# The last chunk of a fused attention and feed-forward kernel: h products first, then output products block by block, with the last block in two halves

## The chip, the cores and the metric

The kernel runs on one core of one Trainium2 chip. The metric is the device time of one execution, in microseconds (us). Engines: PE (TensorE, matmul), DVE (VectorE), ACT (ScalarE), POOL (GpSimd), SP (SyncE, which only issues transfers here).

## The reference, cut to what matters

```python
def reference(q, k, v, w_in, w_out, beta):       # q, k, v: 8 x 8 x 576 x 64
    x = linear_attention(q, k, v)                # cut; gives 4608 tokens x 512
    h = x @ w_in                                 # 512 -> 2048
    g = h * (1.0 / (1.0 + np.exp(-beta * h)))
    return (g @ w_out).astype(np.float32)        # 2048 -> 512
```

## The kernel before

Tokens are handled in 9 chunks of 512. The 2048 columns of `h` make 16 *units* of 128. For each unit, PE makes an `h` product (four matmuls of 128x512 into one PSUM bank), ACT takes a tanh, DVE makes `g`, and PE uses `g` for the *output products*: one matmul for each of four token *blocks* of 128, added up over the 16 units in four PSUM banks `acc0` to `acc3`. At the end each block is copied from PSUM (where matmuls put their results) to SBUF (on-chip memory, from which stores leave) by ACT or DVE, and stored. The code is shortened; `...` marks cuts.

```python
def mm_a(c, j, kts=None, tag=None):              # h product of unit j
    ...                                          # tag "h": two banks; "att": two more
    th = work.tile([P, MAIN], BF16, tag="th", bufs=3)
    nc.scalar.activation(th[:], h[:], ACTF.Tanh, scale=beta_t[:, j : j + 1])
    g = work.tile([P, MAIN], BF16, tag="g", bufs=6)
    nc.vector.scalar_tensor_tensor(out=g[:], in0=th[:], scalar=1.0, in1=h[:], op0=ALU.add, op1=ALU.mult)

def mm_b(c, j, sts=range(R)):                    # output products of unit j, R = 4 blocks
    for st in sts:
        nc.tensor.matmul(acc[st][:], g[:, ds(st * P, P)], w_out_b[:, j, :], start=(j == 0), stop=(j == NJ - 1))

def store(c, st): ...                            # for the last chunk:
    evac(nc.scalar if st in (0, 3) else nc.vector, o[:, st, :], acc[st][:])
    (nc.scalar if st == R - 1 else nc.sync).dma_start(ov[:, st, :], o[:, st, :])

# ... last chunk: h of unit j, output products of unit j - 2, up to j = 13; h of unit 14; then
mm_a(LASTC, NJ - 1, tag="att")
last = [(0, j) for j in range(NJ - 4, NJ - 1)] + [(1, j) for j in range(NJ - 4, NJ - 1)]
last += [(0, NJ - 1), (1, NJ - 1)] + [(st, j) for st in (2, 3) for j in range(NJ - 4, NJ)]
for st, j in last:
    mm_b(LASTC, j, [st])
    if j == NJ - 1:
        store(LASTC, st)
```

The softmax here doesn't subtract the row's maximum and nothing guards it: scores larger than these inputs give would overflow.

## Time and profile before

| | before |
|---|---|
| median of 5 runs | 288.95 us (288.61 to 289.18) |
| profiled span | 286.8 us |
| PE busy | 277.9 us, 97% |
| granted PE clock | full in all 40 slices |

The page of before, its line of PE, its chain of waits by engine, and the two groups of matmuls that fill the time (busy us, mean ns of one, idle time ahead of them and what ended it):

```profile
PE 277.9 (97%) x1595; PEld 127.7 (45%) x1595; DVE 180.0 (63%) x280; ACT 162.9 (57%) x236; POOL 43.7 (15%) x58
...
PE 84%; DMA 11%; SPq 1%; POOL 1%; ACT 1%; issue 0%; DVE 0%; ACTq 0%
...
L358 PE MATMUL h<-xT,w_in_b 128*128 128x512 bf16 x576 | 146.1, 379 | 0.5 <-ACT xT L143 0.2
L386 PE MATMUL acc<-w_out_b,g 128*128 128x512 bf16 x576 | 145.9, 379 | 0.2 <-DVE g L370 0.2
```

PE is the bottleneck nearly everywhere. A group's mean of 379 ns is not the pace: matmuls overlap, and in a stream they start 0.216 us apart.

The timeline of before at its end (start us, duration us, engine, line, what, count; in brackets the idle time before and what ended it):

```profile
276.95 1.89 PE L358 MATMUL h<-xT,w_in_b 128*128 128x512 bf16 x8
277.00 0.69 DVE L370 SCALAR_TENSOR_TENSOR g<-th,h 128x512 bf16<-128x512 bf16 x1 [1.04 <-ACT th L368]
...
278.67 0.60 PE L386 MATMUL acc<-w_out_b,g 128*128 128x512 bf16 x2
278.73 0.69 DVE L370 SCALAR_TENSOR_TENSOR g<-th,h 128x512 bf16<-128x512 bf16 x1 [1.04 <-ACT th L368]
...
279.47 3.20 PE L386 MATMUL acc<-w_out_b,g 128*128 128x512 bf16 x14 [0.20 <-DVE g L370]
...
281.38 1.52 SPq L434 DMA_DIRECT2D out_dram<-o  x3
...
282.71 0.58 ACT L143 COPY o<-acc 128x512 f32<-128x512 f32 x1 [1.36 <-PE acc L386]
283.32 0.37 ACTq L434 DMA_DIRECT2D out_dram<-o  x1
```

At 278.67 PE runs two output products and then needs `g` of unit 14, which DVE ends only at 279.42. The third matmul starts at 279.47 instead of 278.67 + 2 x 0.216 = 279.10: 0.37 us lost. The last block is copied by ACT in 0.58 us, and its store is issued at 283.32.

The windows view of before over its end (window in us, its length, then busy us of PE, PE weight loads, DVE, ACT and POOL, with counts; then granted PE clock, the DMA engines' busy share and GB/s):

```profile
279.00:280.00 1.00, 0.80 (x5) 0.29 (x4) 0.82 (x2) 0.56 (x1) 0.00 (x0) 1.00 0.00 0
...
281.00:282.00 1.00, 1.00 (x6) 0.49 (x5) 0.83 (x2) 0.35 (x1) 0.00 (x0) 1.00 0.00 0
282.00:283.00 1.00, 0.67 (x4) 0.10 (x1) 0.54 (x1) 0.29 (x1) 0.00 (x0) 1.00 0.75 287
283.00:284.00 1.00, 0.00 (x0) 0.00 (x0) 0.00 (x0) 0.29 (x1) 0.00 (x0) 1.00 1.04 371
284.00:285.00 1.00, 0.00 (x0) 0.00 (x0) 0.00 (x0) 0.00 (x0) 0.00 (x0) 1.00 1.00 356
285.00:286.00 1.00, 0.00 (x0) 0.00 (x0) 0.00 (x0) 0.00 (x0) 0.00 (x0) 1.00 0.10 35
```

Before 282 no store of the last chunk moves any data. All four of them (1 MB) are issued within 2 us, from 281.38 to 283.32, and the DMA engines are full (share near 1) until 285. By the trace's packet records the data runs from 282.23 to 285.27, and the last store's own part from 284.29 to 285.27. The span ends 1.56 us after its last byte. The view of this last store (`--tile o --window 283:286.8`) gives the time from its issue to its landing, which is when its completion is signalled:

```profile
DMA to landing us min/median/max: 2.6/2.6/2.6
```

### The profile page before, as it was taken

The numbers are of one execution on the slowest core, as the hardware profiler recorded it, in microseconds if no ns is written. First come the engines' busy times: TensorE is split into PE (matmuls) and PEld (weight loads), VectorE is DVE, ScalarE is ACT, GpSimd is POOL, SyncE is SP. The second block draws the span as 40 slices with busy tenths as digits, with TensorE's granted clock in tenths as the row PEclk, the third lists the DMA queues.
The fourth block names the chain that finished last, engine by engine and source line by source line (L and its number), as shares of the span: only waits on it lengthen the run. The fifth ranks groups of instructions, "written<-read, shape, count | busy, mean of one in ns | idle before, by whom it ended". The sixth has DMA issues, their size and how long they took to land.

```text
span 286.8 us, 4132 instructions
## 1 busy us (share of the span) xinstructions
PE 277.9 (97%) x1595; PEld 127.7 (45%) x1595; DVE 180.0 (63%) x280; ACT 162.9 (57%) x236; POOL 43.7 (15%) x58
## 2 busy tenths in 40 slices
PE   7799999999999999999999999999999999999994
PEld 2444445444444444444444444444445444444441
DVE  7954597695477457855694469456954695464432
ACT  4763586683496448734773568356835563553341
POOL 4458833300030020001200030003000000000000
PEclk9999999999999999999999999999999999999999
DMA  7999999809933963296319911893270033005004
GB/s 242 377 385 387 371 388 321 280 2 264 280 151 76 313 164 146 46 331 175 127 33 270 269 74 76 194 268 119 115 220 2 1 149 73 0 0 149 0 0 146
DMA packets 56227, 50.08 MB, mean 175 GB/s; under 512 B 26240, under 2 KB 47760, under 8 KB 56208
## 3 DMA queue, kind: packets, MB, share of 16 engines
q1 hardware_dynamic: 56064, 49.56, 55.8%
q8 instruction: 12, 0.20, 0.3%
q10 hardware_dynamic: 144, 0.26, 0.3%
q14 instruction: 7, 0.06, 0.1%
HBM read 36.71 MB, written 9.44 MB: 161 GB/s over the span
## 4 chain that ended last, share of the span: by engine, by line
PE 84%; DMA 11%; SPq 1%; POOL 1%; ACT 1%; issue 0%; DVE 0%; ACTq 0%
PE acc L386 40%; PE h L358 39%; DMA w_in<-in_moe_w_in_dram 6%; DMA k_st<-in_k_dram 5%; PE x L314 2%; PE kv L276 2%; POOL w_in_b L145 1%; PE kv L264 0%; PE tp L250 0%; SPq L85 0%; SPq L106 0%; PE x L318 0%; ACT ek L158 0%; DVE g L370 0%; ACT th L368 0%
## 5 line engine op out<-in xcount | busy, mean ns | idle before, releaser
L368 ACT ACTIVATE th<-h,beta_t 128x512 bf16<-128x512 f32 x144 | 98.5, 687 | 102.6 <-PE h L358 100.7
L370 DVE SCALAR_TENSOR_TENSOR g<-th,h 128x512 bf16<-128x512 bf16 x144 | 97.9, 682 | 92.2 <-ACT th L368 90.7
L358 PE MATMUL h<-xT,w_in_b 128*128 128x512 bf16 x576 | 146.1, 379 | 0.5 <-ACT xT L143 0.2
L386 PE MATMUL acc<-w_out_b,g 128*128 128x512 bf16 x576 | 145.9, 379 | 0.2 <-DVE g L370 0.2
L386 PEld LDWEIGHTS <-g 128*128 128x128 bf16 x576 | 56.0, 98 | 67.9 <-DVE g L370 1.0
L358 PEld LDWEIGHTS <-w_in_b 128*128 128x128 bf16 x576 | 55.3, 98 | 67.7 <-issue 2.7
L145 POOL CAST va<-v_st 128x2048 bf16<-128x2048 f32 (+2 forms) x12 | 17.3, 1460 | 145.0 <-DMA v_st<-in_v_dram 145.0
L225 DVE TENSOR_REDUCE rq<-eq 128x16 f32<-128x1024 bf16 x18 | 21.6, 1198 | 2.3 <-ACT eq L214 2.3
L231 DVE TENSOR_TENSOR eq<-eq,rq 128x1024 bf16<-128x1024 bf16 x18 | 22.6, 1257 | 0.1
L214 ACT ACTIVATE eq<-q_st 128x1024 bf16<-128x1024 f32 x16 | 16.3, 1048 | 2.9 <-DMA q_st<-in_q_dram 2.9
L143 ACT CAST xT<-x 128x512 bf16<-128x512 f32 x20 | 11.6, 585 | 11.1 <-PE x L314 10.3
L169 ACT ACTIVATE ek<-k_st 128x1024 bf16<-128x1024 f32 x12 | 12.6, 1047 | 0.0
L145 DVE COPY o<-acc 128x512 f32<-128x512 f32 x18 | 11.6, 683 | 0.9 <-PE acc L386 0.9
L314 PE MATMUL x<-qsT,kvp 128*128 128x512 bf16 x32 | 11.7, 380 | 0.4 <-DVE kvp L309 0.2
L145 DVE CAST xT<-x 128x512 bf16<-128x512 f32 x16 | 10.9, 684 | 0.5 <-PE x L314 0.5
L143 ACT COPY o<-acc 128x512 f32<-128x512 f32 x18 | 9.7, 591 | 2.6 <-PE acc L386 2.6
L158 ACT ACTIVATE ek<-k_st 64x576 bf16<-64x576 f32 x16 | 10.9, 679 | 0.4
L450 PE MATMUL warm<-kvp 128*128 128x512 bf16 x34 | 9.9, 432 | 1.2 <-DVE kvp L478 1.2
L145 POOL CAST w_out_b<-w_out 128x1024 bf16<-128x1024 f32 x8 | 8.2, 1040 | 6.6 <-DMA w_out<-in_moe_w_out_dram 6.5
L309 DVE TENSOR_TENSOR kvp<-kv,rk 64x256 bf16<-64x256 f32 (+2 forms) x24 | 8.0, 333 | 0.6
L145 POOL CAST w_in_b<-w_in 128x1024 bf16<-128x1024 f32 x7 | 7.2, 1040 | 3.5 <-DMA w_in<-in_moe_w_in_dram 3.4
L450 PEld LDWEIGHTS <-kvp 128*128 128x128 bf16 x34 | 3.4, 108 | 5.3 <-issue 2.1
(38 smaller groups left out, 67.1 us busy)
## 6 DMA issues: line engine op xcount, KB each, us to landing
out_dram<-o SPq DMA_DIRECT2D x14, 512.0 KB, 3.4
q_st<-in_q_dram SPq DMA_DIRECT2D x6, 1024.0 KB, 6.5
k_st<-in_k_dram SPq DMA_DIRECT2D x6, 1024.0 KB, 9.1
v_st<-in_v_dram SPq DMA_DIRECT2D x6, 1024.0 KB, 10.5
w_in<-in_moe_w_in_dram SPq DMA_DIRECT2D x3, 1024.0 KB, 9.7
k_st<-in_k_dram SPq DMA_DIRECT2D x8, 288.0 KB, 7.6
q_st<-in_q_dram SPq DMA_DIRECT2D x4, 512.0 KB, 7.8
w_out<-in_moe_w_out_dram SPq DMA_DIRECT2D x4, 512.0 KB, 9.5
```

The lines of the kernel that those rows point to most:

```text
L143: eng.copy(dst, src)
L145: eng.tensor_copy(dst, src)
L169: nc.scalar.activation(ek[b][:, :, h, :].rearrange("p i h d -> p h i d"), k_st[b][:, h, 0 : R * D].rearrange("p h (i d) -> p h i d", i=R), ...
L214: nc.scalar.activation(eq[b][:, :, s * m : (s + 1) * m, :].rearrange("p i h d -> p h i d"), q_st[b][:, s * m : (s + 1) * m, :].rearrange(" ...
L225: nc.vector.tensor_reduce(rq[b][:, 0, :, h], eq[b][:, :, h, :], axis=AX.X, op=ALU.add)
L231: nc.vector.tensor_tensor(eq[b][:, :, h, :], eq[b][:, :, h, :], rq[b][:, 1, :, h].unsqueeze(3).to_broadcast((P, R, m, D)), ALU.mult,)
L314: nc.tensor.matmul(t[:], kvp[:, c, j, :], qsT[c][:, :, j, :])
L358: nc.tensor.matmul(h[:], w_in_b[:, kt, ds(j * P, P)], x_of(c)[:, kt, :], start=(kt == 0), stop=(kt == KT - 1),)
L368: nc.scalar.activation(th[:], h[:], ACTF.Tanh, scale=beta_t[:, j : j + 1])
L370: nc.vector.scalar_tensor_tensor(out=g[:], in0=th[:], scalar=1.0, in1=h[:], op0=ALU.add, op1=ALU.mult)
L386: nc.tensor.matmul(acc[st][:], g[:, ds(st * P, P)], w_out_b[:, j, :], start=(j == 0), stop=(j == NJ - 1),)
L450: nc.tensor.matmul(t[:, 0:cols], kvp[:, B - 1, 0, :], kvp[:, B - 1, :, :].rearrange("p j r -> p (j r)")[:, 0:cols],)
```

## The change

The intent: PE should not wait for the last `g`, the blocks should end one after the other so that each is stored while PE still works on the next, and the last piece to be copied and stored should be small. The `h` products of units 10 to 15 run back to back, the output products of units 8 to 15 are held back and then follow block by block, and block 3 is two halves of 256 columns in two PSUM banks. (The Trainium skill, "PSUM — Partial Sum Buffer", section on bank collisions, says that two engines must not touch one bank's same quadrant at once. That is why the first half can be copied while PE fills the second only if they lie in two banks. The trace of after agrees as far as it goes: the copy of the first half runs from 281.95 to 282.37, and PE works on the second half until 282.79.) The diff, cut to its core:

```diff
-        g = work.tile([P, MAIN], BF16, tag="g", bufs=6, name=f"g{c}_{j}")
+        g = work.tile([P, MAIN], BF16, tag="g", bufs=10, name=f"g{c}_{j}")
 ...
+            if c == LASTC:
+                acc_of[c].append(ps.tile([P, DM], F32, tag="att", bufs=2, name=f"acc{c}_{R}"))
 ...
+            if c == LASTC and st >= R - 1:
+                hw = DM // 2
+                nc.tensor.matmul(
+                    acc[st][:, 0:hw],
+                    g[:, ds((R - 1) * P, P)],
+                    w_out_b[:, j, ds((st - R + 1) * hw, hw)],
+                    start=(j == 0), stop=(j == NJ - 1),
+                )
+                continue
 ...                                         # store(), last chunk
+            if st >= R - 1:
+                ...
+                evac((nc.vector, nc.scalar)[k_], o[:, R - 1, cols], acc[st][:, 0:hw])
+                (nc.sync, nc.scalar)[k_].dma_start(ov[:, R - 1, cols], o[:, R - 1, cols])
+                return
+            evac(nc.scalar if st == 1 else nc.vector, o[:, st, :], acc[st][:])
+            nc.sync.dma_start(ov[:, st, :], o[:, st, :])
 ...                                         # the last chunk's order
+    HOLD = 8
-                mm_a(c, j)
+                mm_a(c, j, tag="att" if n == B and j > HOLD + LAG and j % 3 == 0 else None)
+            if n == B and j >= HOLD + LAG:
+                continue
 ...
-    (the list `last` and its loop)
+    for st in range(R + 1):
+        for j in range(HOLD, NJ):
+            mm_b(LASTC, j, [st])
+        store(LASTC, st)
```

More of the change, by code (lines that the diff above doesn't have):

```diff
@@ L379, in acc_tiles, with mm_b @@
             ]
+            if c == LASTC:
+                acc_of[c].append(ps.tile([P, DM], F32, tag="att", bufs=2, name=f"acc{c}_{R}"))
         return acc_of[c]
-    def mm_b(c, j, sts=range(R)):
+    def mm_b(c, j, sts=None):
         acc = acc_tiles(c)
+        sts = range(len(acc)) if sts is None else sts
         g = g_of[c, j]
         for st in sts:
+            if c == LASTC and st >= R - 1:
[4 more added lines that the diff above has]
+                    w_out_b[:, j, ds((st - R + 1) * hw, hw)],
+                    start=(j == 0),
+                    stop=(j == NJ - 1),
+                )
+                continue
             nc.tensor.matmul(
@@ L430, in store @@
         if c == LASTC:
-            o = stage.tile([P, R, DM], F32, tag="wo", bufs=4, name=f"o{c}_{st}")
-            evac(nc.scalar if st in (0, 3) else nc.vector, o[:, st, :], acc[st][:])
+            if st < R:
+                o_of[c] = stage.tile([P, R, DM], F32, tag="wo", bufs=4, name=f"o{c}_{st}")
+            o = o_of[c]
             ov = out[c * S : c * S + MAIN, :].rearrange("(p i) f -> p i f", i=R)
-            (nc.scalar if st == R - 1 else nc.sync).dma_start(ov[:, st, :], o[:, st, :])
+            if st >= R - 1:
+                hw = DM // 2
+                k_ = st - R + 1
+                cols = ds(k_ * hw, hw)
+                evac((nc.vector, nc.scalar)[k_], o[:, R - 1, cols], acc[st][:, 0:hw])
[3 more added lines that the diff above has]
+            nc.sync.dma_start(ov[:, st, :], o[:, st, :])
             return
@@ L646 @@
         side(1, u)
+    HOLD = 8
     for n in range(1, NCH):
         c = order[n]
-        for j in range(4 if n == 1 else 0, NJ - 1 if n == B else NJ):
+        for j in range(4 if n == 1 else 0, NJ):
             if not (n > 1 and j == 3):
-                mm_a(c, j)
+                mm_a(c, j, tag="att" if n == B and j > HOLD + LAG and j % 3 == 0 else None)
             if n > 1 and j == 2:
                 mm_a(c, 3)
-            if (n, j) == (B, NJ - 2):
-                pass
-            elif j >= LAG:
+            if n == B and j >= HOLD + LAG:
+                continue
+            if j >= LAG:
                 mm_b(c, j - LAG)
@@ L660 @@
             side(n, j)
-    mm_a(LASTC, NJ - 1, tag="att")
-    last = [(0, j) for j in range(NJ - 4, NJ - 1)] + [(1, j) for j in range(NJ - 4, NJ - 1)]
-    last += [(0, NJ - 1), (1, NJ - 1)] + [(st, j) for st in (2, 3) for j in range(NJ - 4, NJ)]
-    for st, j in last:
-        mm_b(LASTC, j, [st])
-        if j == NJ - 1:
-            store(LASTC, st)
+    for st in range(R + 1):
+        for j in range(HOLD, NJ):
+            mm_b(LASTC, j, [st])
+        store(LASTC, st)
 _INS = ['q', 'k', 'v', 'moe_w_in', 'moe_w_out', 'moe_beta']
```

## The prediction

> **What bounds the kernel now.** The page has TensorE (PE) busy 97% of a 286.8 us span at full granted clock; the chain of waits is 84% PE. In the timeline, 259 to 276 us, four 128x512 h products and four output products alternate without a gap, 0.863 us per four, 0.2157 each. So only the tail can change. There (timeline) PE runs block 0's output products of units 12 and 13 at 278.67, then waits for g of unit 14 until 279.47 (0.37 us lost); its last matmul ends at 282.67. ACT copies the last 128x512 block at 282.71 (585 ns); its store is issued at 283.32 and lands 2.6 us later. In the windows view the DMA engines are full (share 0.9 to 1.05) from 282.2 to 285.1: four 256 KB stores are issued at 281.38 to 283.32, closer than they drain (about 0.75 us each). By the packet records the last one's data runs from 284.29 to 285.27; the span ends 1.56 us later.
>
> **What the change does.** PE does the same column work in another order, plus one extra matmul and weight load per unit (16): block 3 becomes two 256-column halves in two banks. Narrow matmuls look cheap: 8 of 128x64 with full weight loads take 0.23 us (timeline, 216.29 to 216.52). The Trainium skill ("TensorE: Matmul & The Clock Gate", Back-to-back issue gap) gives N/2.4 + 2.5 ns when warm, which the 215.7 ns here fits: estimate 16 x 2.5 ns = 0.04 us.
>
> Six h units back to back: from a unit's first matmul to the end of its g is 2.47 us (275.22 to 277.69); with three h banks one is wanted again after 2.59 us. That fits, with 0.1 us to spare. ACT and DVE take 0.69 us per unit against 0.863. Then block 0 needs g of unit 15 seven matmuls, 1.51 us, after the last h product; g is done about 1.6 us after it: a stall of about 0.15 us instead of 0.39. PE ends 0.2 us earlier.
>
> Last eviction, 128x256 on ACT: from 585 ns (512) and 178 ns (16 columns) estimate 0.38 us, 0.2 less. The last store is issued about 282.9.
>
> Stores: blocks end 1.73 us apart (halves 0.87), so each store drains before the next; the last is 128 KB, about 0.4 us of data instead of 0.98. Estimate: 0.95 us from issue to first data, 0.4 of data, 1.56 to the end: 282.93 + 2.9 = 285.85, against 286.83. The Trainium skill ("DMA: Bandwidth & Descriptors", Anatomy of one DMA) has some 2 us of a DMA fixed whatever its size; the two ends here are of that order and do not shrink.
>
> **Sum.** PE stall -0.2, eviction -0.2, last store -0.55: -0.95 us, all on the critical path. 289.15 becomes 288.2 us; range 287.6 to 288.9. Faster by over 2%: 1%; within 2%: 98%; slower: 1%.
>
> **What would show it.** PE stall after the last h product 0.1 to 0.2 us; 256-column matmuls 0.108 to 0.112 us apart; no PE gaps among units 10 to 15; gaps between the last stores; last ACT copy near 0.38 us; last store landing in 2.0 to 2.3 us; nothing changed before 257 us.
>
> **What would make it wrong.** Weight loads not hidden behind 256-column matmuls (98 ns load against 107 ns); bank waits over 2.59 us adding up; 1 KB rows draining slower; run-to-run spread (0.57 us in three runs before) covering the gain.

## The result and the profile after

| | before | after |
|---|---|---|
| median of 5 runs | 288.95 us | 287.87 us (287.68 to 288.50) |
| profiled span | 286.8 us | 286.1 us |

The ratio of after to before is 0.9967, with a 95% interval of 0.9955 to 0.9979. Ratios here compare runs of the same rounds, so they are not quite the ratio of the medians. The gain of about 1 us is clear of the noise.

The page of after, the same lines (the output products are now lines 399 and 391; one line of the whole-kernel list by form is added at the end):

```profile
PE 278.1 (97%) x1611; PEld 129.6 (45%) x1611; DVE 179.8 (63%) x281; ACT 162.7 (57%) x236; POOL 43.5 (15%) x58
...
PE 93%; DMA 4%; SPq 1%; POOL 0%; ACT 0%; DVE 0%; issue 0%
...
L358 PE MATMUL h<-xT,w_in_b 128*128 128x512 bf16 x576 | 145.3, 379 | 1.3 <-POOL w_in_b L145 1.0
L399 PE MATMUL acc<-w_out_b,g 128*128 128x512 bf16 x560 | 141.9, 379 | 0.0
...
L391 PE MATMUL acc<-w_out_b,g 128*128 128x256 bf16 x32 | 5.0, 272 | 0.0
```

There are 16 more matmuls (1611 against 1595). Do not read the chain's rise from 84% to 93% as an effect of the change. The DMA part of the chain fell from 11% to 4%, and its pieces (31.9 us in before, 12.6 in after) all lie in the first 38 us, before any changed instruction. The 1.0 us that PE waited for POOL lies there too; it was 0.2 us in before, and differs from run to run.

The timeline of after at its end:

```profile
270.35 5.34 PE L358 MATMUL h<-xT,w_in_b 128*128 128x512 bf16 x24
...
275.53 5.51 PE L399 MATMUL acc<-w_out_b,g 128*128 128x512 bf16 x24
...
276.45 0.69 DVE L370 SCALAR_TENSOR_TENSOR g<-th,h 128x512 bf16<-128x512 bf16 x1 [0.18 <-ACT th L368]
277.19 3.35 PEld L399 LDWEIGHTS <-g 128*128 128x128 bf16 x17 [0.48 <-DVE g L370]
277.62 0.69 DVE L145 COPY o<-acc 128x512 f32<-128x512 f32 x1 [0.48 <-PE acc L399]
278.34 3.79 SPq L456 DMA_DIRECT2D out_dram<-o  x3
279.35 0.59 ACT L143 COPY o<-acc 128x512 f32<-128x512 f32 x1 [2.93 <-PE acc L399]
...
280.88 1.91 PE L391 MATMUL acc<-w_out_b,g 128*128 128x256 bf16 x16
...
281.95 0.42 DVE L145 COPY o<-acc 128x256 f32<-128x256 f32 x1 [0.18 <-PE acc L391]
282.40 0.33 SPq L453 DMA_DIRECT2D out_dram<-o  x1
282.82 0.37 ACT L143 COPY o<-acc 128x256 f32<-128x256 f32 x1 [2.89 <-PE acc L391]
283.23 0.37 ACTq L453 DMA_DIRECT2D out_dram<-o  x1
```

The 24 `h` matmuls run without a gap: 275.53 - 270.35 = 5.18 us, 24 x 0.216. The 24 whole output products take 280.88 - 275.53 = 5.35 us, 0.17 more than that: the weight load of `g` of unit 15 waits until 277.19. The 16 half-width matmuls start (1.91 - 0.27) / 15 = 0.109 us apart.

The windows view of after:

```profile
279.00:280.00 1.00, 1.00 (x6) 0.42 (x5) 0.00 (x0) 0.59 (x1) 0.00 (x0) 1.00 0.68 262
...
281.00:282.00 1.00, 1.00 (x12) 0.90 (x10) 0.74 (x2) 0.00 (x0) 0.00 (x0) 1.00 0.49 186
282.00:283.00 1.00, 0.79 (x8) 0.46 (x5) 0.38 (x1) 0.18 (x1) 0.00 (x0) 1.00 0.36 139
283.00:284.00 1.00, 0.00 (x0) 0.00 (x0) 0.00 (x0) 0.20 (x1) 0.00 (x0) 1.00 0.71 254
284.00:285.00 1.00, 0.00 (x0) 0.00 (x0) 0.00 (x0) 0.00 (x0) 0.00 (x0) 1.00 0.38 131
285.00:286.00 1.00, 0.00 (x0) 0.00 (x0) 0.00 (x0) 0.00 (x0) 0.00 (x0) 1.00 0.00 0
```

The stores now move data from 279 on, while PE works, and the DMA engines are never full in a whole window. By the packet records the last store's data runs from 284.11 to 284.62, and the span ends 1.48 us later. The view of this last store (`--tile o --window 282.8:286.2`):

```profile
DMA to landing us min/median/max: 1.9/1.9/1.9
```

**A yardstick without the head's noise.** In all 14 profiles, the time from the first tanh of the second chunk to the first tanh of the last chunk is 203.25 to 203.27 us. What precedes it (loading and casting weights) takes 50.57 to 52.44 us, in kernels whose code there is the same. So the spread between these profiled runs lies in the first 50 to 53 us, and the experiments are best compared by the *tail*: from the start of the tanh of unit 2 of the last chunk to the end of the span. Some profiles lack a few matmul records (560 of 576 `h` matmuls), but all 144 tanh records are there, hence this mark. The first experiments' expectations were still counted from the first `h` matmul of unit 2, 1.06 us earlier in both kernels; subtract that.

| run | tanh of unit 2 to end of last matmul | last matmul to end of span | tail | median us | ratio to before |
|---|---|---|---|---|---|
| before | 25.38 | 4.16 | 29.54 | 288.95 | |
| after | 25.20 | 3.31 | 28.52 | 287.87 | 0.9967 |
| e1 order only | 25.17 | 3.96 | 29.12 | 288.56 | 0.9981 |
| e2 split only | 25.42 | 4.41 | 29.83 | 289.54 | 1.0016 |
| e3 hold from 7 | 25.84 | 3.31 | 29.14 | 288.57 | 0.9984 |
| e4 hold from 10 | 26.43 | 3.68 | 30.11 | 289.64 | 1.0026 |
| e5 hold from 7, bank mended | 25.04 | 3.29 | 28.33 | 287.90 | 0.9961 |
| e6 bunched, without effect | 25.20 | 3.31 | 28.51 | 287.97 | 0.9960 |
| e7 quarters | 25.04 | 3.35 | 28.39 | 288.19 | 0.9967 |
| e8 before with 10 g buffers | 25.38 | 4.16 | 29.53 | 289.14 | 1.0003 |
| e9 bunched | 25.20 | 4.58 | 29.79 | 289.13 | 1.0001 |
| e10 384 and 128 | 25.04 | 3.50 | 28.54 | 288.24 | 0.9970 |
| e11 after again | 25.20 | 3.31 | 28.51 | 287.96 | 0.9967 |
| e12 e5 again | 25.04 | 3.31 | 28.35 | 287.95 | 0.9964 |

So the change shortened the tail by 1.02 us: 0.18 on PE and 0.85 after PE's last matmul (rounded separately). The medians differ by 1.08 us.

### The profile page after: what moved, and what is told of

It reads as the page before. It is cut to its first block, busy times and chain, and to the rows that moved or that the text cites. A ratio compares the mean times of both kernels' runs of the same rounds, so it can differ in the third digit from the quotient of the medians.

```text
span 286.1 us, 4169 instructions
## 1 busy us (share of the span) xinstructions
PE 278.1 (97%) x1611; PEld 129.6 (45%) x1611; DVE 179.8 (63%) x281; ACT 162.7 (57%) x236; POOL 43.5 (15%) x58
## 4 chain that ended last, share of the span: by engine, by line
PE 93%; DMA 4%; SPq 1%; POOL 0%; ACT 0%; DVE 0%; issue 0%
PE h L358 44%; PE acc L399 42%; DMA k_st<-in_k_dram 2%; PE x L314 2%; DMA w_in<-in_moe_w_in_dram 2%; PE kv L276 2%; PE acc L391 1%; PE kv L264 1%; PE tp L250 0%; POOL w_in_b L145 0%; SPq L85 0%; PE x L318 0%; ACT xT L143 0%; SPq L106 0%; DVE kvp L309 0%
## 5 line engine op out<-in xcount | busy, mean ns | idle before, releaser
L399 PE MATMUL acc<-w_out_b,g 128*128 128x512 bf16 x560 | 141.9, 379 | 0.0
L399 PEld LDWEIGHTS <-g 128*128 128x128 bf16 x560 | 54.5, 98 | 65.4 <-DVE g L370 0.5
L145 DVE COPY o<-acc 128x512 f32<-128x512 f32 (+1 forms) x19 | 12.1, 669 | 3.4 <-PE acc L399 3.2
L143 ACT COPY o<-acc 128x512 f32<-128x512 f32 (+1 forms) x18 | 9.5, 578 | 5.8 <-PE acc L399 2.9
L169 ACT ACTIVATE ek<-k_st 128x1024 bf16<-128x1024 f32 x12 | 12.6, 1047 | 0.0
```

What stands on the lines that cost most here:

```text
L143: eng.copy(dst, src)
L145: eng.tensor_copy(dst, src)
L169: nc.scalar.activation(ek[b][:, :, h, :].rearrange("p i h d -> p h i d"), k_st[b][:, h, 0 : R * D].rearrange("p h (i d) -> p h i d", i=R), ...
```

## The experiments

The theory: three terms add up. PE waits less (-0.2), the last copy is smaller (-0.2), and the last store is smaller and meets no queue (-0.6). The rivals: only the smaller last piece counts, or only the order does.

### e1: the order alone

```diff
 after, with block 3 in one bank again, copied by ACT, one 256 KB store on ACT's queue:
-    for st in range(R + 1):
+    for st in range(R):
```

> The new order of the last chunk, but block 3 stays one 512-column bank, copied by ACT and stored as one 256 KB store on ACT's queue. Measured from the first h product of unit 2 of the last chunk to the end of the span, before has 30.60 us and after 29.58. Theory (three terms: PE stall -0.2, smaller last eviction -0.2, stores spread and last one smaller -0.6, of which spreading alone -0.25): here the stall is 0.17 us, the last eviction 0.585 us, the last store's data about 0.75 us instead of 0.98, so 30.0 to 30.1 us, ratio to before about 0.998. Rival (the gain is the smaller last piece; order alone gives only the 0.2 us of PE): 30.4 us.

Measured: ratio 0.9981 (0.9969 to 0.9994), tail 29.12 us, 0.42 less than before: 0.21 on PE and 0.20 after it. That is short of the theory's 0.5 to 0.6 and above the rival's 0.2. Its last copy and store in the timeline:

```profile
282.58 0.59 ACT L143 COPY o<-acc 128x512 f32<-128x512 f32 x1 [2.87 <-PE acc L397]
283.19 0.37 ACTq L454 DMA_DIRECT2D out_dram<-o  x1
```

The packet records have the last store's data from 284.06 to 284.89: 0.83 us for 256 KB without a store ahead of it, against 0.98 in before and an expected 0.75. Spreading the stores is thus worth 0.2 us by itself, and PE's order 0.2. Issue to landing of the last store is 2.35 us here, against 2.55 in before.

### e2: the split alone

```diff
 before's order, with block 3 in two halves as in after; block 2 copied by ACT:
-last += [...] + [(st, j) for st in (2, 3) for j in range(NJ - 4, NJ)]
+last += [...] + [(st, j) for st in (2, 3, 4) for j in range(NJ - 4, NJ)]
```

> Before's order of the last units, with block 3 split in two halves (block 2 is copied by ACT so that DVE is free for the first half). Theory: the 1 MB of stores is still bunched and drains in about 3 us from 282.2, so a smaller last piece hardly ends it earlier: 30.35 to 30.5 us from unit 2's first h product to the end (before 30.60), ratio about 0.999. Rival (the smaller last piece is the gain): 29.9 us or less.

Measured: ratio 1.0016 (1.0005 to 1.0028), tail 29.83 us, 0.29 *more* than before. Neither expectation foresaw a loss. The windows view of e2:

```profile
283.00:284.00 1.00, 0.36 (x4) 0.07 (x1) 0.38 (x1) 0.48 (x2) 0.00 (x0) 1.00 1.01 381
284.00:285.00 1.00, 0.00 (x0) 0.00 (x0) 0.00 (x0) 0.00 (x0) 0.00 (x0) 1.00 1.03 358
285.00:286.00 1.00, 0.00 (x0) 0.00 (x0) 0.00 (x0) 0.00 (x0) 0.00 (x0) 1.00 0.84 277
```

The DMA engines are full again. The copy really was shorter (372 ns), and the last store was issued 0.44 us after PE's last matmul instead of 0.65. But its data started only 1.55 us after issue (after: 0.88), behind the bunch, and the whole megabyte took from 282.91 to 286.14, 3.23 us instead of before's 3.04. PE lost another 0.04 us. So here, where the drain is what ends last, a smaller last piece gained nothing. Why the drain was longer is shown only in part. The packet records give 46 ns (median) for a packet of 1 KB, as the half blocks make them, and 84 ns for one of 2 KB; for the 256 KB of block 3, spread over 16 engines, that is 0.06 us more. The other 0.13 us stays open.

Order alone -0.42, split alone +0.29, both -1.02: the split is worth 0.60 us once the stores are spread, and costs 0.29 us while they are bunched. The terms do not simply add. The traces of e1 and after say where the 0.60 us comes from: the last copy is 0.21 us shorter, and the last store lands 1.86 us after issue instead of 2.35, 0.49 less; about 0.1 us is lost elsewhere (PE, and the time after landing).

### e3 and e4: the number of held units

```diff
-    HOLD = 8
+    HOLD = 7        # e3;   HOLD = 10 in e4
```

> After with one output product more held back (units 7 to 15), so that block 0 has 8 matmuls of 0.2157 us ahead of the one that needs g of unit 15. g of unit 15 came 1.66 us after the last h product's matmul began its successor, so the 0.17 us stall should vanish: 29.41 us from unit 2 to the end (after 29.58), no step between PE matmul starts over 0.23 us. Rival (the stall is off the critical path or comes back as bank waits in the longer run of h products): 29.55 to 29.6.

> After with two fewer output products held back (units 10 to 15). Block 0 then has 5 matmuls ahead of the one that needs g of unit 15, so the stall grows by 2 x 0.2157 us from 0.17 to 0.60 us, and blocks end 1.29 us apart instead of 1.73 (halves 0.65): 29.95 to 30.05 us from unit 2 to the end, if stores do not collide; up to 0.2 more if they do. Rival (the held count does not matter, the gain is only in the split): 29.6.

Both missed. e3's tail is 29.14 us (ratio 0.9984, 0.9972 to 0.9996), and e4's 30.11 us (ratio 1.0026, 1.0010 to 1.0042). The timeline of e3 shows why:

```profile
269.25 1.89 PE L358 MATMUL h<-xT,w_in_b 128*128 128x512 bf16 x8
...
271.03 0.69 DVE L370 SCALAR_TENSOR_TENSOR g<-th,h 128x512 bf16<-128x512 bf16 x1 [1.04 <-ACT th L368]
...
271.77 2.10 PE L358 MATMUL h<-xT,w_in_b 128*128 128x512 bf16 x9 [0.64 <-DVE g L370]
```

PE's step from 270.756 to 271.771 is 1.015 us, where 0.216 is the rule: 0.80 us lost, until DVE has ended a `g` at 271.72. The change gives the third `h` bank to units with `j % 3 == 0`, which fits a run that begins at unit 10. With the run moved by one or two units, an `h` product came only two units after the one whose bank it needs (unit 11 in e3, unit 14 in e4). This was an error of the edit, not of the held count. In numbers, e3's PE part is after's 25.20 + 0.80 for the bank - 0.16 for the vanished wait on unit 15 = 25.84, as measured. e4's is 25.20 + 0.80 + 0.43 (its wait for `g` of unit 15: a step of 0.804 us against after's 0.372) = 26.43, as measured. e4 also lost 0.37 us after PE's end. Its last store was issued as soon as in after (0.44 us after PE's end) and drained as fast (0.52 us of data), but it landed 0.80 us after its last byte, where after has 0.46. Its stores are closer together (the first three are issued 1.2 and 1.4 us apart, in after 1.6 and 1.8); that this delays the landing is likely, but not shown. The rival of e4, that the held count does not matter, falls.

### e5 and e12: hold from unit 7, with the third bank in place

```diff
-    HOLD = 8
+    HOLD = 7
-                mm_a(c, j, tag="att" if n == B and j > HOLD + LAG and j % 3 == 0 else None)
+                mm_a(c, j, tag="att" if n == B and j > HOLD + LAG and (j - HOLD - LAG) % 3 == 2 else None)
```

> e3 with the third h bank in its place: units 11 and 14 of the run (its third and sixth) use it, not 12 and 15, so that no h product comes two units after one whose bank it needs. Theory (e3's step of 1.015 us at unit 11 was a wait for a bank that g of unit 9 still read, an accident of my edit, and its g-of-15 stall was gone): no step between PE matmul starts over 0.23 us; from the tanh of unit 2 of the last chunk to the end 28.35 us (after 28.52, e3 29.14, before 29.54). Rival (a longer run stalls by itself, e.g. on g buffers): about 29.1 again.

> e5 again, beside the changed kernel: 28.33 us from the tanh of unit 2 to the end, 0.19 under the changed kernel's; the ratio of the two in whole time about 0.9993, which is less than the spread of the runs resolves.

Measured: tails of 28.33 and 28.35 us, 0.16 to 0.19 less than after, nearly all of it on PE (25.04 against 25.20). The PE steps over 0.23 us that remain in both traces are of 0.432 us, twice 0.216: places of a missing record, not of a wait. The timeline of e5:

```profile
274.80 5.99 PE L399 MATMUL acc<-w_out_b,g 128*128 128x512 bf16 x27
```

27 matmuls in one stream: 26 x 0.216 + 0.38 = 5.99 us, so nothing is lost here. This confirms the account of e3, and that the wait for the last `g` is on the critical path. The ratios, 0.9961 (0.9948 to 0.9973) and 0.9964 (0.9951 to 0.9976), are not distinct from after's.

### e6 and e9: stores bunched on purpose

```diff
 after, in store(), blocks 1 and 2 of the last chunk:
-            nc.sync.dma_start(ov[:, st, :], o[:, st, :])
+            late.append((ov[:, st, :], o[:, st, :]))
 e6: `late` is issued ahead of the first half's store; e9: behind it
```

> After with the stores of blocks 1 and 2 held back and issued just ahead of the first half of block 3; all computing is as in after. Theory (the last store queues behind whatever is still draining, about 345 GB/s): 640 KB are issued from 282.4 on, so the last 128 KB end about 2.2 us after the first data (282.4 + 0.9), near 285.5 instead of 284.62: from the tanh of unit 2 to the end 29.2 to 29.5 us (after 28.52). Rival (store spacing does not matter, only the last piece's own size): 28.5 to 28.65.

> e6 done right (there the held-back stores still left as soon as their data was ready, since only their place in the program had moved): the queue now issues the first half of block 3 first and blocks 1 and 2 behind it, so these cannot leave before 282.4 in after's times. All computing is as in after. Theory (stores drain at about 345 GB/s in the order they come; what is bunched at the end is paid for): 768 KB from 283.3 on end near 285.5 instead of 284.62: 29.3 to 29.5 us from the tanh of unit 2 of the last chunk to the end (after 28.52). Rival (the fixed ends of a store hide the draining): under 28.8.

e6 changed nothing (tail 28.51 us), and says nothing about the theory. Its edit moved the calls in the program but not their order on SP's queue, and the stores of blocks 1 and 2 were still issued as soon as their copies had ended, at 279.85 and 281.69 (in after at 279.96 and 281.80). e9 put them behind a store that has to wait. Computing is as in after (25.20 us), and the tail is 29.79 us, 1.27 more; the ratio to before is 1.0001 (0.9986 to 1.0016). The windows view of e9:

```profile
281.00:282.00 1.00, 1.00 (x11) 0.90 (x10) 0.69 (x1) 0.00 (x0) 0.00 (x0) 1.00 0.00 0
...
283.00:284.00 1.00, 0.00 (x0) 0.00 (x0) 0.00 (x0) 0.26 (x1) 0.00 (x0) 1.00 0.58 203
284.00:285.00 1.00, 0.00 (x0) 0.00 (x0) 0.00 (x0) 0.00 (x0) 0.00 (x0) 1.00 0.97 356
285.00:286.00 1.00, 0.00 (x0) 0.00 (x0) 0.00 (x0) 0.00 (x0) 0.00 (x0) 1.00 0.59 227
```

Blocks 1 and 2, which in after are out by 283.47, now drain together with the two halves: 768 KB (786,432 bytes) from 283.31 to 285.72, 326 GB/s. The loss is larger than the 0.8 to 1.0 expected; the rival falls. Bunching takes back the whole gain of the change. But e9 does one thing more: the store that ends last is now one of 256 KB. It landed 3.08 us after issue; e1's lone store of 256 KB took 2.35 us and after's of 128 KB 1.86. So of the 1.27 us some 0.7 is the queue and some 0.5 the size of the store that ends last.

### e7 and e10: a still smaller last piece

```diff
 e7, on e5: the last 256 columns copied as 128 by DVE and 128 by ACT, stored from two queues
+    for x, (e1, e2) in enumerate(((nc.vector, nc.sync), (nc.scalar, nc.scalar))):
+        evac(e1, o2[x][:, R - 1, c1], acc[st][:, x * hw // 2 : (x + 1) * hw // 2])
+        e2.dma_start(ov[:, R - 1, c1], o2[x][:, R - 1, c1])
 e10, on e5: block 3 split 384 and 128
+    lo, hw = ((0, 384), (384, 128))[st - R + 1]
```

> e5 with the last 256 columns copied as 128 by DVE and 128 by ACT at once and stored from two queues, 64 KB each. Theory (a smaller last piece shortens the eviction by about 0.09 us, its data by up to 0.1, if 512-byte rows drain as fast): 28.15 to 28.3 us from the tanh of unit 2 to the end. Rival (fixed costs and slower small rows eat it): 28.35 or more.

> e5 with block 3 split 384 and 128 columns in place of 256 and 256. Theory: the last piece is copied in 0.27 instead of 0.37 us and is 64 KB, but the 192 KB ahead of it are issued only 0.2 us before it, so both drain together, 256 KB in 0.75 us: 28.2 to 28.35 us from the tanh of unit 2 to the end (e5 28.33). Rival (only the last piece's size counts): 28.05 or less.

e7 measured 28.39 us, e10 28.54: neither beats e5. In e7 the two copies did not run at once, as its timeline shows:

```profile
283.36 0.29 DVE L145 COPY o<-acc 128x128 f32<-128x128 f32 x1 [0.56 <-PE acc L391]
...
283.69 0.27 ACT L143 COPY o_last<-acc 128x128 f32<-128x128 f32 x1 [3.65 <-DVE o L145]
```

Both read one bank, and ACT was made to wait for DVE. This agrees with what the Trainium skill ("PSUM — Partial Sum Buffer", section on bank collisions) says of two engines on one bank, reads included. So e7 tested a serial copy, and whether a parallel one would pay stays open. In e10 the 384 columns took DVE 0.56 us, so their store was issued only 0.2 us before the last; the two drained together and the tail was 0.2 us longer than e5's. The theory said up to 28.35, so it was too low; the result fits its point that the piece ahead of the last must be out of the way.

### e8 and e11: controls

```diff
 e8, on before:
-        g = work.tile([P, MAIN], BF16, tag="g", bufs=6, name=f"g{c}_{j}")
+        g = work.tile([P, MAIN], BF16, tag="g", bufs=10, name=f"g{c}_{j}")
 e11: after, unchanged
```

> Before with ten g buffers in place of six and nothing else. All theories: 29.54 us from the tanh of unit 2 to the end, ratio 1.000 within 0.002. If the ratio leaves that, the buffers' place in memory itself acts on the time and the other ratios need correcting for it.

> The changed kernel unchanged, on the chip of the two next to it: 28.52 us again from the tanh of unit 2 to the end, ratio to before 0.996 to 0.9975.

e8: ratio 1.0003 (0.9988 to 1.0018), tail 29.53 us. The buffers' number and place do not act on the time, as far as this resolves. e11: ratio 0.9967 (0.9955 to 0.9980), tail 28.51 us, on another chip. The best version found is e5: 0.16 us less than after in the tail, side by side on one chip (e12 and e11), which whole times do not resolve (287.95 against 287.96 us).

## Why the prediction was right

It said 288.2 us (287.6 to 288.9), and 287.87 us was measured. Its tail of -0.95 us measured -1.02. About 0.2 us of the difference in absolute time is that it started from 289.15 us, the median of three runs of before, where five runs have 288.95.

- *PE stall 0.15 instead of 0.39 us, PE ends 0.2 us earlier:* right. Steps of 0.372 and 0.585 us between PE starts mean waits of 0.16 and 0.37; PE's part fell by 0.18. e5 and e3 show that the wait is real and on the path.
- *Narrow matmuls cost 0.04 us in all:* right. Seven units of the last chunk (tanh of unit 2 to that of unit 9) take 12.104 us instead of 12.086, so 2.6 ns each and 0.04 us for 16. The Trainium skill's N/2.4 + 2.5 ns ("TensorE: Matmul & The Clock Gate", Back-to-back issue gap) gives, by our working, 109.2 ns for 256 columns; the trace has 0.109 us.
- *No gaps among units 10 to 15:* right. The prediction counted three banks; it did not say that the count is not enough. e3 shows that a third bank one unit too late costs 0.80 us.
- *Last eviction 0.38 us, 0.2 less:* right (372 ns against 585).
- *Last store -0.55 us:* right in kind, a little small. From issue to the end of the span, before has 286.83 - 283.32 = 3.51 us, and after 286.10 - 283.23 = 2.87: -0.64. Data took 0.52 us, not the estimated 0.4, but issue to first data fell from 0.96 to 0.88 and the rest after the last byte from 1.56 to 1.48, which the prediction had kept fixed at 0.95 and 1.56. These errors (+0.12, -0.07, -0.08 us) nearly cancel, and that they do is luck. The store landed in 1.9 us, below the stated 2.0 to 2.3; from last byte to landing the time fell from 0.61 to 0.46 us.
- *What it did not see:* it added up the terms as if each stood alone. e1, e2 and e9 show that the split pays only with the spread stores.
- *The spread between runs:* rightly named as a risk. In the profiled runs all of it lies before the changed code.

## What to carry to other kernels

In the tail of a kernel that PE bounds, look at what drains after the last matmul: let blocks finish one after the other, far enough apart that each store is out before the next, and only then make the last piece small. Shrinking the last piece while its queue was full lost time here (e2). When a run of products rotates over a few banks, check that each comes back in time at every position of the run, and compare variants by a stretch of the trace that excludes the noisy part.

## What the Trainium skill lacked or had wrong

- "TensorE: Matmul & The Clock Gate", Back-to-back issue gap: it gives about 131 ns per matmul for sustained pairs of weight load and matmul at N = 512, and calls N/2.4 + 2.5 ns an isolated figure. Here hundreds of such pairs run 215.7 ns apart, and 256-column pairs 109 ns: the "isolated" formula is the sustained pace of this kernel.
- The same page, LDWEIGHTS: it gives P/1.2 ns, by our working 107 ns for 128 columns. The records of the two large groups show 98 ns.
- "DMA: Bandwidth & Descriptors", Anatomy of one DMA: the fit of 2.0 us plus bytes/436e3 is for transfers issued from GpSimd and would give, by our working, 2.3 us for 128 KB and 2.6 us for 256 KB. A store from ACT's queue with nothing queued ahead landed in 1.86 us with 128 KB (after) and in 2.35 us with 256 KB (e1): less, but with a larger step from one size to the other (0.49 us against 0.3). No page gives such a fit for the SP and ACT queues, or for what queued stores add (issue to first data 0.88 us alone, 1.55 us in e2).
